# A spectral gate with a token-mixing MLP: two interruptions of the first output pair exchanged

## The chip, the cores and the metric

The kernel runs on one core of one Trainium2 chip. The metric is the device time of one execution in microseconds (us); lower is better. The kernel before has a median of 364.88 us over 3 runs (364.87 to 364.95). The engines are named as the profile names them: PE is TensorE (matmuls; PEld is its weight loads), DVE is VectorE, ACT is ScalarE, POOL is GpSimd, and SP is SyncE, which only issues DMAs.

## The reference

```python
x = A_x                                   # (1, S=2048, D=512)
xn = _layernorm(x, axis=-1)
X = rfft2(xn) * (w_r + 1j * w_i)          # over tokens and channels
s = irfft2(X)                             # (1, 2048, 512)
u = gelu(einsum("bsd,sf->bdf", _layernorm(xn), w1) + b1)    # F = 1792
y = einsum("bdf,fs->bds", u, w2) + b2
g = silu(y.transpose(0, 2, 1))
return x + s * g
```

So there are two branches on the normalised tokens: a two-dimensional Fourier filter `s`, and an MLP across the tokens whose output, through silu, gates it.

## The kernel before, in words

The tokens lie in 16 groups of 128 (`NJ`), each a tile of 128 partitions by 512 channels. The work goes through three stages.

In the first, each group is normalised, the first products of the MLP (`w1` against the tokens, 128x512 matmuls in three passes of high and low parts) run, and between them the transform over the tokens. In the second, the remaining products of `w1` run, and eight steps of the spectral filter (`filter_pair`) are put between them. Its result stays in the tile `ey`, still without the last transform over the channels.

The third stage makes the output, and the change lies there. The 16 output groups are taken as 8 pairs `p`, groups `p` and `p + 8`. Each pair's share of `w2 * u` is a 2x2 block product, and it is made with seven products instead of eight, in the order `ORDER = (1, 2, 5, 6, 3, 7, 4)`. The product `n` (`products`, line 905) is 21 matmuls of 128x128 by 256 columns: three passes (high by high, high by low, low by high) over seven blocks (`FORMS`). The fixed side comes from a weight form `w2f`, of which there are three buffers: ACT copies its high part, DVE makes its low part (`w2_high`, `w2_low`). The moving side is one of the stored forms of `u`, `fa` to `fd`. Products 1, 6, 7 and 4 go to one bank of PSUM (bank 3 for even pairs, bank 2 for odd ones), product 2 to bank 4, products 5 and 3 to bank 5.

Between the products stands the last transform of the spectral branch, in small steps that I call interruptions:

- `gathered` (line 953) copies a pair's columns of `ey` into the tile `yt`, two copies on ACT and two on DVE.
- `even_channels` (line 966) multiplies `yt` with the constants `ci` for the even channels: 16 fp32 matmuls on 64x64 quarters of the array, 32 records in the profile, into the first 256 columns of banks 6 and 7.
- `odd_channels` (line 977) does the same for the odd channels: 4 fp32 matmuls on the full array, 8 records, into the last 256 columns of these banks.
- `unfolded` (line 984) has ACT copy a part of bank 7 and DVE add and subtract the two into `es` and `y`.
- `spectral` (line 1006) is the last step over the tokens: 4 fp32 matmuls on quarters (8 records) from `y` into banks 0 and 1. `finish` multiplies with the gate and adds to the output.

The order of the work is written out by hand: `tc.keep_in_program_order` keeps each engine's instructions as the program issues them. For the loop over `k` (line 1047) `SLOTS` says behind which product a pair's interruption stands (`slot`; 6 for the first pair, which is the seventh product, 5 for most others), and which pieces of `gathered` and `unfolded` follow each product. `PARTS` (line 44) says what the interruption holds and in which order: S is `spectral` of the pair before, E the even channels, O the odd ones. The first pair alone has its transform in two interruptions: line 1074 puts a step behind the sixth product, `k == slot - 1`, and `PARTS[0]` names the one behind the seventh. The second pair and the last have "SEO", the five between them "ESO". `even_channels` and `odd_channels` of a pair write different columns, and `unfolded` comes behind both.

Of the kernel before, what the change touches and what calls it, by code (L numbers as in the profile page):

```python
# [40 lines left out]

PARTS = ("O", "SEO", *["ESO"] * 5, "SEO")

KD = np.concatenate([np.arange(0, 256, 4), np.arange(2, 256, 4), np.arange(1, 256, 2)])

# [94 lines left out]
def spectral_mixer_kernel(tc, x, w1, b1, w2, b2, wk, we, wx, c_f, c_ft, c_d, c_i, c_g, c_h, out):  # L142
# [19 lines left out]
    with tc.tile_pool(name="ps", bufs=1, space=PSUM) as psp, ExitStack() as left, ExitStack() as right:  # L162
# [675 lines left out]
        def sums_of_blocks():  # L838
            added_up("a12", "s1")
            added_up("a11", "a12")  # L840
# [61 lines left out]
        def banks(p):  # L902
            return ps[:, 3 - p % 2, :HD], ps[:, 4, :HD], ps[:, 5, :HD]

        def products(p, n):

            wf = ready.pop(0)
            bx, by, bz = banks(p)
            o = {1: bx, 6: bx, 7: bx, 4: bx, 2: by, 5: bz, 3: bz}[n]

            for a, (wi, ui) in enumerate(((0, 0), (0, 1), (1, 0))):
                for m, i in enumerate(FORMS):
                    T.matmul(o, wf[:, wi, i], form_parts(n, i)[ui], start=m + a == 0 and n in (1, 2, 5),
                             stop=m == NH - 1 and a == 2, skip_group_check=n in (6, 3, 7, 4))

        def copied(name, src, where):
            t = where.tile([P, HD], F32, name=name, tag=name.split("_")[0], bufs=1)
            step(A.activation(t, src, AF.Copy))
            return t
# [25 lines left out]
        def new_gates(p):  # L945
            return [fp.tile([P, D], F32, name=f"g{j}", tag="g", bufs=4) for j in (p, p + NP)]
# [6 lines left out]
        def gathered(p):  # L953


            yt = fp.tile([P, 2, 4, 2, 64], F32, name=f"yt{p}", tag="yt")
            yts[p] = yt
            for i, j in enumerate((p, p + NP)):
                for h in range(2):
                    to = yt[:, i, :, h ^ i].rearrange("p b (s c) -> p b s c", c=2)  # L960
                    yield V.tensor_copy(to, ey[:, :, h::2, j]) if i else A.activation(to, ey[:, :, h::2, j], AF.Copy)

        def tokens_of(yt, i, b):
            return yt[:, i, b].rearrange("p e c -> p (e c)")

        def even_channels(p):


            for i in range(2):
                for s in range(2):  # L970
                    at = slice(128 * i + 64 * s, 128 * i + 64 * s + 64)
                    for e in range(2):
                        for r, rows in enumerate((slice(0, 64), slice(64, P))):
                            T.matmul(ps[64 * e:64 * e + 64, 6 + r, at], yts[p][rows, i, 2 * s, e], ci[rows, 2 * s, :64],
                                     start=True, stop=True)

        def odd_channels(p):

            for i in range(2):
                for s in (1, 0):  # L980
                    at = 256 + 128 * s
                    T.matmul(ps[:, 6 + i, at:at + P], tokens_of(yts[p], i, 2 * s + 1), ci[:, 2 * s + 1], start=True, stop=True)

        def unfolded(p):

            es, y = new_sums(p) if p else first_sums
            e0, e1 = (es[:, :, k].rearrange("p i b c -> p i (b c)") for k in range(2))
            first, odd = ps[:, 6, :256].rearrange("p (i s c) -> p i s c", s=2, c=64), ps[:, 6:8, 256:]
            other = y.rearrange("p i h q c -> p (i h q c)")[:, :257]
            A.activation(other, ps[:, 7, :257], AF.Copy)  # L990
            other = other[:, :256].rearrange("p (i s c) -> p i s c", s=2, c=64)

            V.tensor_add(es[:, :, 1, :, :64], first, other)
            V.tensor_sub(es[:, :, 1, 0, :63:-1], first[:, :, 0], other[:, :, 0])
            V.tensor_sub(es[:, :, 1, 1, :63:-1], other[:, :, 1], first[:, :, 1])
            V.tensor_add(e0, e1, odd)
            V.tensor_sub(e1, e1, odd)
            yield
            u, v = es[:, :, :, 0], es[:, :, :, 1]
            V.tensor_add(y[:, :, :, 0], u, v)  # L1000
            yield
            V.tensor_sub(y[:, :, ::-1, 1], u, v)
            ys[p] = y.rearrange("p i h q c -> p i (h q c)")
            yield

        def spectral(p):

            y = ys.pop(p)
            for e, cols in enumerate((slice(0, 64), slice(64, P))):
                for r, rows in enumerate((slice(0, 64), slice(64, P))):  # L1010
                    i = e ^ r
                    T.matmul(ps[cols, i], cft[rows, cols], y[rows, i], start=True, stop=True)

        def gate(g, j, cols, src, scale):
            A.activation(g[:, cols], src, AF.Silu, bias=b2t[:, j:j + 1], scale=scale)

        def summed(name, a, b):
            t = fp.tile([P, HD], F32, name=name, tag="c", bufs=2)
            V.tensor_add(t, a, b)
            return t  # L1020
# [17 lines left out]
        for p in range(NP):  # L1038
            j0, j1 = p, p + NP
            more = p + 1 < NP  # L1040
            if p:
                gates[p] = new_gates(p)
            g0, g1 = gates[p]
            bx, by, bz = banks(p)
            slot, plan = SLOTS[min(p, 2) + (not more)]
            gathering = gathered(p)
            for k, n in enumerate(ORDER):
                started = not p and k < 2
                if not started:
                    products(p, n)  # L1050
                if n == 1 and p:
                    p1 = copied(f"p1_{p}", bx, w2p)
                elif n == 5:
                    p5 = copied(f"p5_{p}", bz, fp)
                elif n == 6:
                    v2 = copied(f"v2_{p}", bx, fp)
                elif n == 7:
                    c22 = summed(f"c22_{p}", bx, p5)
                if n == 3 and more:
                    c12 = summed(f"c12_{p}", bz, v2)  # L1060
                if not started:
                    ready.extend(w for w in [next(wforms, None)] if w is not None)
                if n == 2:
                    c11 = summed(f"c11_{p}", by, p1)
                elif n == 6:
                    gate(g0, j0, left_, c11, 1.0)
                elif n == 3 and more:
                    gate(g0, j0, right_, c12, 1.0)
                elif n == 7:
                    gate(g1, j1, right_, c22, -1.0)  # L1070
                elif n == 4:
                    for cols in (left_,) if more else quarter_rows:
                        gate(g1, j1, cols, bx[:, cols], -1.0)
                if not p and k == slot - 1:
                    even_channels(p)
                if k == slot:
                    for part in PARTS[p]:
                        {"S": spectral, "E": even_channels, "O": odd_channels}[part](p - (part == "S"))
                    yts.pop(p)
                    pieces = unfolded(p)  # L1080
                    if p:
                        for g, j in zip(gates.pop(p - 1), (j0 - 1, j1 - 1)):
                            finish(g, j, whole)
                for what in plan.get(k, ""):
                    next(gathering if what == "g" else pieces)
                if n == 3 and not more:
                    gate(g0, j0, right_, summed(f"c12_{p}", bz, v2), 1.0)
                if more and n == 7:
                    sums_of_blocks()
                if not more and k == 2:  # L1090
                    xr = [where.tile([P, NH * P], F32, name=f"xr{i}", tag="s1", bufs=1)[:, :D] for i, where in enumerate((w2p, fp))]
                    for to, j in zip(xr, (j0, j1)):
                        for rows, tokens in halved:
                            SY.dma_start(to[rows], x[tokens, j])
                if not more and k == 5:
                    spectral(p)
                    last_rows = fp.tile([P, 2, D], F32, name="rows", tag="yt")
                    finish(g0, j0, whole)
                    finish(g1, j1, right_)
# [38 lines left out]
```

## Time and profile before

| what | value |
|---|---|
| median of 3 runs | 364.88 us (364.87 to 364.95) |
| the profiled execution's own time | 365.01 us |
| its span, first to last instruction | 363.2 us |
| mean granted TensorE clock | 0.996 |
| busy PE, PEld | 357.3 us, 310.4 us |
| busy DVE, ACT, POOL | 307.4 us, 210.8 us, 87.2 us |
| HBM traffic | 59.70 MB read, 8.13 MB written |

A line of the timeline gives the start from the beginning of the span, the length, the engine, the line, the operation with its tiles (output first, then inputs) and how many instructions are merged in it; in brackets stands how long the engine sat idle before it and what ended that. The line is 139 for nearly all, because a helper on that line issues them; so the tiles tell the steps apart. `ps<-fb,w2f` is a product, `ps<-cd,yt 64*64` the even channels, `ps<-cd,yt 128*128` the odd ones, `ps<-y,cft` the step over the tokens. In a merged line the matmuls overlap; the length runs to the end of the last one. Where two kinds of work follow each other with the same tiles, one line holds both ("x40" is 32 records of even and 8 of odd channels).

### The profile page before, as it was taken

To read this page: it belongs to the slowest core of one execution; us is meant where nothing else is said; L and a number is where in the kernel's file an instruction comes from. 1 tells how busy PE (TensorE), PEld (TensorE's weight loads), DVE (VectorE), ACT (ScalarE), POOL (GpSimd) and SP (SyncE) were. 2 spreads that over 40 slices of the span, in tenths; PEclk is the share of its full clock that TensorE was granted. 3 is DMA by queue.
4 is the path that set the end of the run, shared out by engine and by line. 5 is a ranking of instruction groups with operands and counts; after the bars stand their busy time and mean duration, and the time that the engine had idled before them with its cause. 6 is when DMAs were issued, how large, how long until landed. Compare 5 with 4: busy or idle time off the path is not lost.

```text
span 363.2 us, 8851 instructions
## 1 busy us (share of the span) xinstructions
PE 357.3 (98%) x3476; PEld 310.4 (85%) x3476; DVE 307.4 (85%) x590; ACT 210.8 (58%) x385; POOL 87.2 (24%) x134
## 2 busy tenths in 40 slices
PE   8999999999999999999999999999999999999994
PEld 7788888888777788777888999999898989898993
DVE  5899999967799996999995988687887878787974
ACT  4877778867534425756337884646464546565431
POOL 4233333323222022220120001050504132230330
PEclk9999999999999999999999999999999999999998
DMA  7978999306695686996568288698888989898624
GB/s 211 253 181 205 219 289 317 143 0 158 174 264 188 192 249 178 253 239 208 175 213 181 101 227 174 180 188 203 195 192 203 188 216 175 233 151 219 113 27 90
DMA packets 33293, 68.66 MB, mean 189 GB/s; under 512 B 4612, under 2 KB 19380, under 8 KB 33124
## 3 DMA queue, kind: packets, MB, share of 16 engines
q1 hardware_dynamic: 24276, 42.44, 41.2%
q0 software_dynamic: 8496, 25.01, 32.1%
q10 hardware_dynamic: 480, 0.66, 0.6%
q8 instruction: 27, 0.44, 0.5%
q14 instruction: 14, 0.11, 0.1%
HBM read 59.70 MB, written 8.13 MB: 187 GB/s over the span
## 4 chain that ended last, share of the span: by engine, by line
PE 97%; DMA 1%; DVE 1%; ACT 0%; issue 0%; DVEq 0%
PE ps L139 97%; DMA x<-in_x_dram 1%; DVE rows L139 0%; DVE stm L244 0%; DVE h L272 0%; ACT g L139 0%; DVE tm L229 0%; ACT sdm L223 0%; DVEq L1134 0%; DVE mvm L220 0%; DVE rsm L230 0%; DVE r0m L228 0%; DVE v2m L221 0%; DVE v2m L222 0%; DVEq L469 0%
## 5 line engine op out<-in xcount | busy, mean ns | idle before, releaser
L139 PE MATMUL ps<-h,w1h 128*128 128x512 f32 x400 | 116.3, 397 | 0.3 <-DVE h L272 0.3
L139 PEld LDWEIGHTS ps<-h,w1h 128*128 128x128 f32 x400 | 72.9, 188 | 20.1 <-issue 4.9
L139 PE MATMUL ps<-h,w1l 128*128 128x512 f32 x200 | 67.6, 390 | 0.0
L139 DVE TENSOR_TENSOR w2f<-a,w2f 128x896 fp32r<-128x896 f32 x36 | 39.2, 1090 | 16.4 <-ACT w2f L139 16.4
L139 ACT ACTIVATE w2f<-a 128x896 fp32r<-128x896 f32 x36 | 37.1, 1030 | 19.8 <-ACT g L139 8.4
L139 PEld LDWEIGHTS ps<-h,w1l 128*128 128x128 f32 x200 | 37.5, 188 | 8.1
L139 PE MATMUL ps<-fb,w2f 128*128 128x256 f32 x336 | 41.9, 279 | 0.0
L139 POOL DMA_DIRECT2D s<-in_w_dram x14 | 18.3, 1311 | 96.5 <-DVE w2f L139 46.5
L139 PE MATMUL ps<-fa,w2f 128*128 128x256 f32 x336 | 41.2, 277 | 0.0
L139 PEld LDWEIGHTS ps<-fb,w2f 128*128 128x128 f32 x336 | 39.7, 188 | 0.9 <-DVE c L139 0.8
L139 PE MATMUL ps<-fc,w2f 128*128 128x256 f32 x336 | 39.8, 277 | 0.0
L139 PEld LDWEIGHTS ps<-fa,w2f 128*128 128x128 f32 x336 | 39.7, 188 | 0.0
L139 PEld LDWEIGHTS ps<-fc,w2f 128*128 128x128 f32 x336 | 39.0, 188 | 0.0
L155 ACT ACTIVATE w1h<-w1s 128x512 fp32r<-128x512 f32 x26 | 16.2, 631 | 25.1 <-DMA w1s<-in_w_dram 12.0
L139 POOL DMA_DIRECT2D out_dram<-r x28 | 23.6, 1276 | 26.7 <-DVE r L139 26.7
L667 POOL DMA_DIRECT2D xc<-xc x16 | 9.8, 620 | 70.3 <-ACT xc L665 55.1
L308 POOL TENSOR_TENSOR ey<-t 128x256 f32<-128x256 f32 x16 | 15.7, 980 | 44.0 <-DVE t L306 44.0
L139 ACT ACTIVATE w2f<-s 128x896 fp32r<-128x896 f32 x15 | 15.3, 1020 | 14.1 <-PE ps L139 12.3
L139 DVE TENSOR_TENSOR w2f<-s,w2f 128x896 fp32r<-128x896 f32 x15 | 16.3, 1089 | 6.2 <-ACT w2f L139 6.1
L469 DVE TENSOR_TENSOR w1l<-w1r,w1h 128x384 fp32r<-128x384 f32 x32 | 21.3, 670 | 0.0
L268 ACT ACTIVATE h<-x,nbm,rsm 128x256 f32<-128x256 f32 (+1 forms) x34 | 18.4, 591 | 4.2 <-DVE nbm L263 3.2
L139 PE MATMUL ps<-fd,w2f 128*128 128x256 f32 x168 | 20.6, 277 | 0.0
(132 smaller groups left out, 602.1 us busy)
## 6 DMA issues: line engine op xcount, KB each, us to landing
a<-in_w_dram SPq DMA_DIRECT2D x22, 448.0 KB, 4.2
wt<-in_wk_dram POOLq DMA_DIRECT2D x16, 512.0 KB, 6.1
s<-in_w_dram SPq DMA_DIRECT2D x16, 448.0 KB, 4.5
s<-in_w_dram POOLq DMA_DIRECT2D x16, 448.0 KB, 6.7
w1s<-in_w_dram SPq DMA_DIRECT2D x52, 128.0 KB, 5.0
w1r<-in_w_dram SPq DMA_DIRECT2D x28, 192.0 KB, 4.6
xc<-xc POOLq DMA_DIRECT2D x16, 256.0 KB, 3.1
out_dram<-in_x_dram SPq DMA_DIRECT2D x4, 960.0 KB, 6.7
```

The source lines that it names most:

```text
L139: return lambda *args, **kw: self.keep(operation(*args, **kw))
L155: return A.activation(hi, src, AF.Copy), V.tensor_sub(lo, src, hi.bitcast(F32))
L268: keep(A.activation(to, v, AF.Identity, bias=m["nb"][:, i], scale=m["rs"][:, i, 1:2]))
L308: G.tensor_add(ey[:, 0::3, :, j], a, b)
L469: keep(V.tensor_sub(dst, src, hi.bitcast(F32)))
L667: keep(G.dma_start(*(v.rearrange("p s t c -> p s (t c)") for v in (there[c::2], here[1 - c::2, ::-1]))))
```

## The change

The two interruptions of the first pair change places: the odd channels stand behind the sixth product (`n` = 7), the even channels, on the quarters of the array, behind the seventh (`n` = 4). The other pairs, the pieces of `gathered` and `unfolded`, and all other instructions stay as they are.

```diff
-PARTS = ("O", "SEO", *["ESO"] * 5, "SEO")
+PARTS = ("E", "SEO", *["ESO"] * 5, "SEO")
...
                 if not p and k == slot - 1:
-                    even_channels(p)
+                    odd_channels(p)
                 if k == slot:
                     for part in PARTS[p]:
                         {"S": spectral, "E": even_channels, "O": odd_channels}[part](p - (part == "S"))
```

## The prediction

> **What bounds the kernel now.** I read the page of the profile first (busy shares), then the chain that ended last in order of time, then the waits of TensorE (PE in the profile), then PE's timeline through the output stage, and last the other engines around the two places that the change touches.
>
> ```profile
> PE 357.3 (98%) x3476; PEld 310.4 (85%) x3476; DVE 307.4 (85%) x590; ACT 210.8 (58%) x385; POOL 87.2 (24%) x134
> ...
> 199.88 158.78 PE ps L139 x1573
> ...
> PE ps L139 <- POOL wz L443: 1.1, 1, 1.1
> PE ps L139 <- DVE h L272: 0.3, 1, 0.3
> ```
>
> The second line is the chain: from 199.88 us it is PE alone for 158.78 us, through the whole output stage up to 4 us before the end. The last two lines are all that PE waited for by that view, both at the start of the kernel (the zero tile, the first normalised rows). So the time here is the sum of PE's own steps, and a change to the order of two of them counts only if it changes that sum or makes PE wait. PE's timeline around the two interruptions is therefore the place to work from. The columns are start, length, engine, line, operation and count.
>
> ```profile
> 212.56 2.64 PE L139 MATMUL ps<-fa,w2f 128*128 128x256 f32 x21
> 215.03 2.63 PE L139 MATMUL ps<-fb,w2f 128*128 128x256 f32 x21
> 217.59 0.69 PE L139 MATMUL ps<-cd,yt 64*64 64x64 f32 x32
> 218.22 2.74 PE L139 MATMUL ps<-fb,w2f 128*128 128x256 f32 x21
> 220.80 1.05 PE L139 MATMUL ps<-cd,yt 128*128 128x128 f32 x8
> 221.61 2.72 PE L139 MATMUL ps<-fd,w2f 128*128 128x256 f32 x21
> 224.16 2.63 PE L139 MATMUL ps<-fa,w2f 128*128 128x256 f32 x21
> ```
>
> A row of 21 matmuls is one product. Lengths overlap, because matmuls are pipelined, so I take a step's cost from its start to the next step's start. The fifth product (212.56) takes 2.47 us in this way with product on either side: that is a plain product. The sixth takes 2.56, the even channels (32 records on 64x64 quarters) 0.63, the seventh 2.58, the odd channels (8 records on the full array) 0.81, and the first product of the next pair 2.55.
>
> **The change part by part.** The change exchanges the rows at 217.59 and 220.80 and nothing else. No matmul is added or removed, no DMA is issued by either step, and the queues of SP and POOL are not passed: both steps hold matmuls only. VectorE (DVE) and ScalarE (ACT) keep their order.
>
> Step 1, the sum on PE as it is: 2.56 + 0.63 + 2.58 + 0.81 + 2.55 = 9.13 us from 215.03 to 224.16. Three plain products are 3 x 2.47 = 7.41, so the two interruptions cost 1.72. Of that 0.63 + 0.81 = 1.44 is their own; 0.09 lies at the edge into the even channels (2.56 against 2.47), 0.11 in the product between the even and the odd channels (2.58), which I count to the even channels' exit, 0.08 behind the odd channels (2.55).
>
> Step 2, the sum after: each interruption still stands between two products of the same shape, so each keeps its edges: 2.47 + 0.81 + 2.47 + 0.08 + 0.09 + 0.63 + 2.47 + 0.11 = 9.13. The difference is 0.00. The one edge that moves to an unseen neighbour is that behind the even channels, with the first product of the next pair behind it instead of the seventh of this one. Its nearest row is the edge of 0.11 above. Taken from nothing to twice that, the cost is bounded at -0.11 and +0.11; I take 0.00, since the two products have the same shape and count.
>
> Step 3, waits of the moved step. The odd channels now start where the even ones did, 3.21 us earlier (220.80 - 217.59). They read the gathered tile yt, and need both halves of its rows, but so do the even channels.
>
> ```profile
> 214.35 0.78 ACT L139 ACTIVATE yt<-ey 128x256 f32<-128x256 f32 x2
> 215.39 0.54 DVE L139 COPY yt<-ey 128x256 f32<-128x256 f32 x2
> ...
> 221.04 1.05 ACT L139 ACTIVATE w2f<-s 128x896 fp32r<-128x896 f32 x1 [1.86 <-issue]
> ...
> 222.01 0.46 ACT L139 ACTIVATE g<-ps,b2t 128x256 f32<-128x256 f32 x1
> 222.13 1.09 DVE L139 TENSOR_TENSOR w2f<-s,w2f 128x896 fp32r<-128x896 f32 x1
> 222.36 0.37 ACT L139 ACTIVATE y<-ps 128x257 f32<-128x257 f32 x1
> ...
> 229.28 0.68 DVE L139 TENSOR_TENSOR y<-es 128x512 f32<-128x512 f32 x1
> ```
>
> The four copies are over at 215.93 (215.39 + 0.54), 1.66 us ahead of 217.59, so the odd channels find them done. If that cover were gone, each microsecond that the copies are late would be a microsecond of PE.
>
> Step 4, what follows later. The seventh product ended 2.56 + 0.63 + 2.58 = 5.77 us behind 215.03; it will end 2.47 + 0.81 + 2.47 + 0.08 = 5.83 behind it, 0.06 later, or 0.15 if the edge of 0.09 into the even channels is counted in. ACT's copy of a new weight form at 221.04 waits for that product to give back its buffer, since there are three such buffers; behind it on ACT stand the gate at 222.01 and the copy at 222.36 that starts the unfolding. All three slip by at most 0.15. The low half of that form, on DVE, ends at 223.22 (222.13 + 1.09), and by the code's order its product is the third of the next pair. That one and PE's next reader of the unfolded y are in these rows:
>
> ```profile
> 226.64 5.11 PE L139 MATMUL ps<-fc,w2f 128*128 128x256 f32 x42
> ...
> 234.06 2.63 PE L139 MATMUL ps<-fb,w2f 128*128 128x256 f32 x21
> 236.62 1.09 PE L139 MATMUL ps<-y,cft 64*64 64x512 f32 x8
> 237.53 1.73 PE L139 MATMUL ps<-cd,yt 64*64 64x64 f32 x40
> 239.02 2.63 PE L139 MATMUL ps<-fb,w2f 128*128 128x256 f32 x21
> 241.49 2.54 PE L139 MATMUL ps<-fd,w2f 128*128 128x256 f32 x21
> 243.87 2.54 PE L139 MATMUL ps<-fa,w2f 128*128 128x256 f32 x21
> 246.25 4.92 PE L139 MATMUL ps<-fc,w2f 128*128 128x256 f32 x42
> ```
>
> The form has 3.42 us to spare (226.64 - 223.22), the unfolded y 6.66 (236.62 - 229.96). A slip of 0.15 is hidden in both, at no cost. Were those margins gone, PE would wait 0.15.
>
> The sum is 0.00, with -0.11 to +0.11 for the moved edge. Against the profiled execution's own time of 365.01 us (a span of 363.2 and 1.8 around it) it leaves 365.01; that execution stands 0.13 above the median of 364.88, so the forecast in terms of the median is 364.88, given as 364.9.
>
> **The rivals.** The first has to do with a thing in these rows that the sum passes over: the plain product has two prices. Before 236.62 it is 2.47; from 241.49 on it is 2.38 (243.87 - 241.49, and again 246.25 - 243.87). The step between them falls on an interruption, and so does the step back near the end:
>
> ```profile
> 340.07 2.54 PE L139 MATMUL ps<-fa,w2f 128*128 128x256 f32 x21
> 342.45 4.92 PE L139 MATMUL ps<-fc,w2f 128*128 128x256 f32 x42
> 347.30 1.09 PE L139 MATMUL ps<-y,cft 64*64 64x512 f32 x8
> 348.21 1.73 PE L139 MATMUL ps<-cd,yt 64*64 64x64 f32 x40
> 349.70 2.72 PE L139 MATMUL ps<-fa,w2f 128*128 128x256 f32 x21
> 352.26 2.63 PE L139 MATMUL ps<-fb,w2f 128*128 128x256 f32 x21
> 354.89 1.09 PE L139 MATMUL ps<-y,cft 64*64 64x512 f32 x8
> ```
>
> At 340.07 a product is still 2.38 (342.45 - 340.07); at 349.70 it is 2.56, which is 2.47 and the 0.08 behind odd channels. So a product costs about 0.09 us more or less according to how PE came out of the interruption ahead of it, and it stays so until the next one.
>
> The Trainium skill bears on that: its page "TensorE: Matmul & The Clock Gate", section "Back-to-back issue gap", gives one gap for an isolated matmul of 256 columns, N / 2.4 + 2.5 = 109.2 ns, and says that in a real stream weight load and matmul set the spacing together, through a reorder window of 64. The first half by itself would leave no room for two prices and give this rival no chance. This trace disagrees with a single figure (2.47 / 21 = 118 ns and 2.38 / 21 = 113 ns); the second half leaves room for a rhythm that an interruption can set.
>
> Rival 1: the exchanged order sets the quicker rhythm earlier. What speaks for it: at 239.02 the quick rhythm begins with odd channels that are followed directly by a seventh product, and the new order makes just that pairing behind the sixth product of the first pair. Against it: odd channels followed by another product have left it slow (221.61, 349.70), and those at 239.02 come behind other 64x64 work, not behind a product. If it holds from the seventh product of the first pair up to 236.62, 7 products gain 0.09 each: 7 x 0.09 = 0.63, and the time is 364.25. If the even channels, after which it was slow at 218.22, put it back at once, the gain is one product, 0.09, and the time 364.79; I count that under the forecast, in whose range it lies.
>
> Rival 2, slower: the interruption in pair 1 (236.62 to 239.02) turns the rhythm over rather than setting it. The interruption of the same order at 347.30 did turn it from quick to slow. If rival 1's condition holds, so that PE enters 236.62 quick, it would then leave it slow, and the products of the next pairs, whose interruptions have kept the rhythm they found, stay slow until 347.30. That is 1 + 5 x 7 + 4 = 40 products at 0.09, 3.60 lost, less the 0.63 won ahead and 3 x 0.09 = 0.27 if the last interruptions turn it over too: 2.70 slower, 367.58. It decides at the product at 241.49. Against it: the two interruptions of that order stand before different products, so that one setting is as good a reading as one turning over.
>
> Rival 3: the 0.15 of step 4 eats into a margin that I have not seen, and PE waits for a weight form or for y. It would need a margin more than twenty times smaller than the 3.42 above, and would give at most 364.88 + 0.15 = 365.03.
>
> **How the numbers follow.** A measurement of this kernel can tell about 0.2% (0.73 us) from no change. Forecast, no change on PE (364.77 to 364.99): 0.70. Rival 1: 0.19. Rival 2: 0.06. Rival 3: 0.05. The forecast, rival 3 and nearly all of rival 1 lie within 0.73 us. Rival 1 with the edge's best bound comes to 0.63 + 0.11 = 0.74, just beyond, and I give 0.03 to that; slower takes the 0.06 of rival 2 and 0.01 of rival 3 for a price larger than its bound. So faster is 0.03, same 0.90, slower 0.07. The range goes from rival 1's 364.25, rounded down to 364.2, to rival 3's 365.03, rounded up to 365.1, and leaves out rival 2.
>
> **What would show it right or wrong.** Right: in the changed profile the odd channels' row stands near 217.5, the even channels' near 221.0, the first product of the second pair ends as before, so that 224.16 reappears within 0.1, and the plain product is 2.47 up to the second pair's interruption and 2.38 behind it. Rival 1 shows as 2.38 between the two interruptions, or from there up to the second pair's, and a row of 236.62 that comes up to 0.63 earlier. Rival 2 shows as 2.47 at 241.49 and after. Rival 3 shows as a wait of PE for DVE or ACT near 226 or 236. The prediction is wrong if the time differs by more than 0.2%; step 2 is wrong if the five steps from 215.03 no longer sum to 9.13 within 0.11.

## The result and the profile after

The changed kernel is slower: 366.45 us (median of 5 runs, 366.25 to 366.78) against 364.88. The ratio is 1.0041, with a 95% interval of 1.0028 to 1.0053: some 1.5 us, clear of no change. The profiled execution took 366.78 us, with a span of 365.0; that of before 365.01 with 363.2.

The page's busy shares say little: PE is busy 1.4 us longer and its share is 98% as before. The first two lines are from the page, the others from the waits of PE.

```profile
span 365.0 us, 8851 instructions
...
PE 358.7 (98%) x3476; PEld 311.4 (85%) x3476; DVE 307.5 (84%) x590; ACT 211.1 (58%) x385; POOL 87.1 (24%) x134
...
PE ps L139 <- POOL wz L443: 1.1, 1, 1.1
PE ps L139 <- DVE h L272: 0.3, 1, 0.3
PE ps L139 <- DVE c L139: 0.2, 1, 0.2
```

The third wait is new, PE for a sum `c` on DVE. PE's timeline shows where it stands, and the rest of the loss.

```profile
215.07 2.63 PE L139 MATMUL ps<-fb,w2f 128*128 128x256 f32 x21
217.55 1.05 PE L139 MATMUL ps<-cd,yt 128*128 128x128 f32 x8
218.81 2.74 PE L139 MATMUL ps<-fb,w2f 128*128 128x256 f32 x21 [0.22 <-DVE c L139]
221.49 0.69 PE L139 MATMUL ps<-cd,yt 64*64 64x64 f32 x32
222.11 2.74 PE L139 MATMUL ps<-fd,w2f 128*128 128x256 f32 x21
...
234.58 2.63 PE L139 MATMUL ps<-fb,w2f 128*128 128x256 f32 x21
237.15 1.09 PE L139 MATMUL ps<-y,cft 64*64 64x512 f32 x8
238.06 1.73 PE L139 MATMUL ps<-cd,yt 64*64 64x64 f32 x40
239.54 2.72 PE L139 MATMUL ps<-fb,w2f 128*128 128x256 f32 x21
242.10 2.63 PE L139 MATMUL ps<-fd,w2f 128*128 128x256 f32 x21
244.58 2.63 PE L139 MATMUL ps<-fa,w2f 128*128 128x256 f32 x21
...
278.41 1.16 PE L139 MATMUL ps<-cd,yt 128*128 128x128 f32 x8
279.33 2.63 PE L139 MATMUL ps<-fb,w2f 128*128 128x256 f32 x21
281.80 2.54 PE L139 MATMUL ps<-fd,w2f 128*128 128x256 f32 x21
284.18 2.54 PE L139 MATMUL ps<-fa,w2f 128*128 128x256 f32 x21
```

I number the pairs from 0, as the code does. Against before, the start of the step over the tokens in pair 1 is 0.53 late (237.15 against 236.62): 0.05 was there before the interruption (217.55 against 217.50, see e2), and the odd channels with the wait take 1.26 (218.81 - 217.55) where the exchange alone takes 0.81, which is 0.45; the last 0.03 lie in the product behind the wait. Nothing is added up to 239.54 (239.02 before). Then it grows. In before the product is quick, 2.38, from 241.49 on; here it is slow, 2.48 (244.58 - 242.10), and turns quick only behind the interruption of pair 3. These are before's rows there:

```profile
276.59 1.16 PE L139 MATMUL ps<-cd,yt 128*128 128x128 f32 x8
277.50 2.63 PE L139 MATMUL ps<-fb,w2f 128*128 128x256 f32 x21
```

279.33 against 277.50 is 1.83 late, and so it stays: the last product starts 1.81 later (357.72 against 355.91). So 1.83 - 0.52 = 1.31 us went between 239.54 and 279.33, over 14 products: 0.093 each, the difference between the two prices. The granted clock has no part in it: it is 1.00 in that stretch in both kernels (columns: window; its length, PE busy and instructions; granted clock; DMA share; GB/s). First the kernel before, then the changed one.

```profile
241.00:276.00 35.00, 35.00 (x363) 1.00 0.85 194
```

```profile
241.00:276.00 35.00, 35.00 (x325) 1.00 0.82 179
```

In the same 35 us PE is busy throughout, at the same clock. The two counts, 363 and 325, are not the price of a product: most of the 38 more in before are small matmuls of pair 3's interruption, which begins at 275.10 there and at 276.93, outside the window, in the changed kernel. The products alone show it: 279 of their matmuls in 31.84 us of PE's time in before, 277 in 32.67 in the changed kernel, about 114 against 118 ns each.

The wait has its cause in DVE's and ACT's rows.

```profile
216.27 1.03 ACT L139 ACTIVATE w2f<-a 128x896 fp32r<-128x896 f32 x1 [1.09 <-DMA a<-in_w_dram]
217.33 1.09 DVE L139 TENSOR_TENSOR w2f<-a,w2f 128x896 fp32r<-128x896 f32 x1 [1.04 <-ACT w2f L139]
218.34 0.42 DVE L139 TENSOR_TENSOR c<-ps,p 128x256 f32<-128x256 f32 x1
```

The sum `c22` reads bank 3 behind the sixth product, and the seventh goes on accumulating into the same bank, so it has to wait until `c22` has read. `c22` stands on DVE behind the low part of pair 1's first weight form, that behind ACT's copy, and that waited for a weight load until 216.27. In before the load came 0.60 earlier:

```profile
215.67 1.03 ACT L139 ACTIVATE w2f<-a 128x896 fp32r<-128x896 f32 x1 [0.54 <-DMA a<-in_w_dram]
...
217.75 0.42 DVE L139 TENSOR_TENSOR c<-ps,p 128x256 f32<-128x256 f32 x1
```

There `c22` was over at 218.17, 0.05 ahead of the seventh product at 218.22. That 0.05 is no margin: where PE did wait, it started just as far behind the sum's end (here 218.34 + 0.42 = 218.76 and 218.81).

### The profile page after: what moved, and what is told of

Its sections match the earlier page's. It is cut to its first block, busy times and chain, and to the rows that moved or that the text cites. A ratio compares the mean times of both kernels' runs of the same rounds, so it can differ in the third digit from the quotient of the medians.

```text
span 365.0 us, 8851 instructions
## 1 busy us (share of the span) xinstructions
PE 358.7 (98%) x3476; PEld 311.4 (85%) x3476; DVE 307.5 (84%) x590; ACT 211.1 (58%) x385; POOL 87.1 (24%) x134
## 4 chain that ended last, share of the span: by engine, by line
PE 91%; DMA 3%; DVE 2%; ACT 2%; issue 1%; ACTq 1%; DVEq 0%; SPq 0%
PE ps L139 91%; DMA a<-in_w_dram 2%; DMA w1r<-in_w_dram 1%; DVE a L836 1%; ACTq L452 1%; ACT fc L363 0%; ACT h L268 0%; ACT w2f L139 0%; DVE w2f L824 0%; ACT w2f L820 0%; DVE rows L139 0%; DVE h L469 0%; ACT u L355 0%; DVE fc L368 0%; DVE fa L368 0%
```

## The experiments

I call the price that holds from product to product the rhythm: slow at 2.47, quick at 2.38. Three theories stood at the start: the wait for `c22` costs the time and upsets the rhythm too (W+R in the expectations); the order of the two steps sets the rhythm, wait or no wait (O); the wait is chance, a load that lands late, in either kernel (L). The tables come first. The ratio is that to the kernel before, run beside each.

| run | edit | median us | ratio (95%) |
|---|---|---|---|
| e1 | the kernel before | 365.03 | 1.0002 (0.9989 to 1.0016) |
| e2 | the changed kernel | 366.29 | 1.0031 (1.0021 to 1.0042) |
| e3 | changed, `c22` first on DVE | 366.31 | 1.0031 (1.0019 to 1.0043) |
| e4 | odd, even, both behind the sixth product | 366.31 | 1.0030 (1.0019 to 1.0041) |
| n1 | changed, 2 extra matmuls in pair 1 | 368.91 | 1.0104 (1.0089 to 1.0120) |
| n2 | before, 2 extra matmuls in pair 1 | 366.48 | 1.0039 (1.0026 to 1.0051) |
| n3 | changed, 1 extra | 368.73 | 1.0097 (1.0082 to 1.0112) |
| n4 | changed, 3 extra | 365.32 | 1.0005 (0.9996 to 1.0015) |
| v1 | even, odd, both behind the sixth product | 364.94 | 0.9997 (0.9988 to 1.0007) |
| c1 | before, 2 extra at the stage's start | 366.54 | 1.0038 (1.0023 to 1.0053) |
| w1 | pair 0's both behind the sixth product, pairs 1 to 6 even-step-odd, 1 extra | 368.77 | 1.0091 (1.0076 to 1.0107) |
| w2 | the same, 2 extra | 369.01 | 1.0097 (1.0076 to 1.0118) |
| e5 | before, `c22` first on DVE | 364.97 | 0.9991 (0.9979 to 1.0003) |

The second table tests the account. "Shift" is how much later than in before (234.06) pair 1's sixth product starts, with any extra work behind it and any wait at the end; "slow" is how many more slow products than in before follow, up to the end. The very last product counts too: it is slow in before (the row at 355.91 is 2.74 long) and quick in the changed kernel (2.65 at 357.72), so the 14 above are 13 here. The sum is 363.2 + shift + 0.093 x slow.

| run | shift | slow | sum | span |
|---|---|---|---|---|
| after | 0.52 | 13 | 364.9 | 365.0 |
| e1 | 0.46 | 0 | 363.7 | 363.7 |
| e2 | 0.00 | 13 | 364.4 | 364.5 |
| e3 | 0.01 | 14 | 364.5 | 364.5 |
| e4 | 0.11 | 14 | 364.6 | 364.6 |
| v1 | 0.40 | 0 | 363.6 | 363.6 |
| e5 | -0.14 | 0 | 363.1 | 363.1 |
| n1 | 0.04 + 0.18 + 0.17 | 38 | 367.1 | 367.2 |
| n2 | -0.01 + 0.18 | 14 | 364.7 | 364.7 |
| n3 | -0.06 + 0.07 + 0.16 | 38 | 366.9 | 366.9 |
| n4 | 0.07 + 0.29 | -1 | 363.5 | 363.5 |
| c1 | 0.23 | 14 | 364.7 | 364.8 |
| w1 | 0.22 + 0.18 | 37 | 367.0 | 367.1 |
| w2 | 0.23 + 0.17 | 38 | 367.1 | 367.2 |

So the shift and the number of slow products together give every span to 0.1 us, and most of the difference lies in the second. (The fourteenth run, s1, doesn't fit the table; see there.)

**The two kernels again, and the wait taken away.** e1 and e2 are the two kernels unchanged. e3 is the changed kernel with `c22` ahead of that low part on DVE, which takes the wait away by order:

```diff
-                yield w2_form(f"1_{p}", cur["a12"])
+                w = w2_high(f"1_{p}", cur["a12"])
+                if p == 1:
+                    yield
+                yield w2_low(*w)
...
                     c22 = summed(f"c22_{p}", bx, p5)
+                    if not p:
+                        ready.append(next(wforms))
```

> The kernel before once more, for a second profile. Theory W+R (the seventh product waits for DVE's sum c22, and a wait of PE upsets the rhythm of later products): 364.9 us, no wait of PE behind the first matmul stage, the plain product 2.47 us up to pair 1's interruption and 2.38 from there to the last pair. Rival L (the wait only comes from weights that happened to land late, whatever the order): the seventh product waits here as well in some executions, times spread by about 0.5 us.

> The changed kernel once more. W+R: 366.2 to 366.8 us, a wait of the seventh product of pair 0 for DVE of 0.1 to 0.6 us, and the quick rhythm (2.38) beginning in another pair than in its first profile or in the same, since the wait ends at no fixed moment. Rival O (the order of odd and even channels sets the rhythm, wait or no wait): the quick rhythm begins at the same place as in its first profile, pair 3's interruption. Rival L: in an execution with the weights on time 364.9.

> The changed order, but DVE makes the sum c22 ahead of the low part of pair 1's first weight form, so that it no longer stands behind a weight load. W+R: the wait is gone (c22 ends near 218.1, the odd channels at 218.4), 364.9 us with a spread below 0.1, and the rhythm of the kernel before. Rival O: no wait, but the slow rhythm up to pair 2 or 3 stays, 365.6 to 366.3 us. Rival L: 364.9 as well, but so would the changed kernel in e2 with its weights on time.

The timeline of e1, the kernel before:

```profile
216.14 1.03 ACT L139 ACTIVATE w2f<-a 128x896 fp32r<-128x896 f32 x1 [0.93 <-DMA a<-in_w_dram]
...
218.21 0.42 DVE L139 TENSOR_TENSOR c<-ps,p 128x256 f32<-128x256 f32 x1
218.68 2.74 PE L139 MATMUL ps<-fb,w2f 128*128 128x256 f32 x21 [0.31 <-DVE c L139]
```

And PE's timeline of e2, the changed kernel:

```profile
215.03 2.63 PE L139 MATMUL ps<-fb,w2f 128*128 128x256 f32 x21
217.50 1.05 PE L139 MATMUL ps<-cd,yt 128*128 128x128 f32 x8
218.31 2.72 PE L139 MATMUL ps<-fb,w2f 128*128 128x256 f32 x21
220.96 0.69 PE L139 MATMUL ps<-cd,yt 64*64 64x64 f32 x32
221.59 2.74 PE L139 MATMUL ps<-fd,w2f 128*128 128x256 f32 x21
224.17 2.63 PE L139 MATMUL ps<-fa,w2f 128*128 128x256 f32 x21
...
237.53 1.73 PE L139 MATMUL ps<-cd,yt 64*64 64x64 f32 x40
239.02 2.72 PE L139 MATMUL ps<-fb,w2f 128*128 128x256 f32 x21
241.58 2.63 PE L139 MATMUL ps<-fd,w2f 128*128 128x256 f32 x21
244.06 2.63 PE L139 MATMUL ps<-fa,w2f 128*128 128x256 f32 x21
```

The wait changes sides: the kernel before has it here, the changed kernel hasn't. With it e1 is as quick behind pair 1 as before; without it e2 and e3 (whose waits name no `c`) are as slow as the changed kernel was. So the wait comes and goes with the landing of a load, as L has it, costs its own 0.4 us or so, and isn't what made the difference: W+R, and L too, gave 364.9 for a changed kernel free of the wait, and it took 366.3. e2 shows that difference bare: 224.17, 237.53 and 239.02 stand where before has 224.16, 237.53 and 239.02, and then one product takes 2.56 where it took 2.47. From pair 1 on both programs give PE the same instructions with the same operands.

**Order or place.** Is it the order, odd before even? e4 puts both steps behind the sixth product in that order, v1 in the other one, with nothing behind the seventh:

```diff
-PARTS = ("E", "SEO", *["ESO"] * 5, "SEO")
+PARTS = ("", "SEO", *["ESO"] * 5, "SEO")
...
                 if not p and k == slot - 1:
                     odd_channels(p)
+                    even_channels(p)
```

(v1 has `even_channels(p)` ahead of `odd_channels(p)`.)

> Odd and then even channels both behind the sixth product, none behind the seventh. The cover of the sum c22 is then 0.81 + 0.6 us. W+R: no wait, or one below 0.1, 364.8 to 364.9 us (one edge of 0.1 fewer), small spread. Rival O: no wait, slow rhythm up to pair 2 or 3, 365.5 to 366.2. Rival L: 364.8.

> No extra matmul: even and then odd channels of pair 0, both behind the sixth product. The sum c22 has 1.5 us of cover. Theory G: no forecast of the pair of turning from the order alone; the time is 364.8 + 0.093 for each slow product more, or less, than in the kernel before (364.3 if the quick rhythm begins behind this interruption, 364.9 in pair 1, 366.2 in pair 3, 368.7 never). Rival O (odd ahead of even is what costs): even ahead of odd, so as the kernel before, 364.8 to 364.9.

e4 has no wait for `c` either and turns quick at pair 3 like the changed kernel, v1 at pair 1 like the one before. Had these been the last runs, "the odd channels must come last" would have looked shown. It was not, as the next runs tell.

**A few matmuls more.** If the order as such sets the rhythm, a little extra work on PE ahead of pair 1's interruption leaves it alone. The extra matmuls are 128x128 by 128 columns, with forms at hand; their result is read by nothing:

```diff
+        def nudge(n, m, wf):
+            for _ in range(m):
+                T.matmul(ps[:, 4, HD:HD + P], wf[:, 0, FORMS[0]],
+                         form_parts(n, FORMS[0])[0][:, :P], start=True, stop=True, ...)
...
                 if k == slot:
+                    nudge(n, NUDGE.get((p, "x"), 0), last[0])
                     for part in PARTS[p]:
```

Theory G in the expectations is a guess of mine from the starts in the traces: the moment at which PE enters an interruption, taken on a grid of a few nanoseconds, decides how it leaves. `NUDGE` gives the number of extra matmuls for pair 1 (n1 and n2: 2, n3: 1, n4: 3); c1 has 2 ahead of pair 0's first product instead. n2 and c1 are the kernel before otherwise, n1, n3 and n4 the changed one.

> The changed order, with two extra 128-column matmuls on the full array (their result is used by nobody) behind the sixth product of pair 1, ahead of that pair's interruption. Theory G (the rhythm after an interruption depends on the moment at which PE enters it, on a fine grid of some 6.7 ns; in e1 to e4 that moment followed from the order alone, wait or no wait): two matmuls at a start distance of about 111.7 ns shift the moment by 3.3 ns on that grid, which is what separates the quick from the slow case of pair 1, so the quick rhythm begins in pair 1, about 14 products gain 0.093 each, 1.3 less 0.22 for the two: 365.1 to 365.3 us. Rival O (the order of odd and even channels in pair 0 keeps it slow up to pair 3 by itself): 366.2 + 0.2 = 366.4 to 366.5 us.

> The order of before, with the same two extra matmuls at the same place. Theory G: pair 1 now comes out of its interruption slow, as in the changed kernel, and the quick rhythm begins some pairs later: 364.9 + 0.2 + up to 1.3, so 365.7 to 366.4 us. Rival O: quick from pair 1 as before, 364.9 + 0.2 = 365.1 us.

> The changed order with one extra matmul of 128 columns (result unused) ahead of pair 1's interruption, where n1 had two and stayed slow from pair 1 to pair 6. Theory G (the moment of entry on a fine grid sets the rhythm): another moment, so another pair in which the quick rhythm begins, or none; the time is 364.9 + 0.15 for the extra matmul + 0.093 for each slow product more than the kernel before has, between 365.0 and 368.9 us, and differs from the 366.4 that the extra matmul alone would make of the changed kernel, unless the moment happens to lead to pair 3 again. Rival O (the order by itself keeps it slow up to pair 3): 366.4 us.

> The same with three extra matmuls. Theory G: again its own pair of turning, 365.3 to 369.1 us, by 364.9 + 0.38 + 0.093 for each further slow product. Rival O: 366.65 us.

> The order of before with two extra matmuls ahead of the very first product of the output stage. Theory G: the moment of the whole stage is shifted, so the pair of turning may be another one, and the first products may be quick from the start: 365.1 if nothing turns, 363.9 if the 13 products ahead of pair 1's interruption become quick and the rest stays, 366.4 to 367.5 if they do but pair 1 leaves slow. Rival O: 365.1.

PE's timeline behind pair 1's interruption in n2, the kernel before with two matmuls more:

```profile
239.18 2.72 PE L140 MATMUL ps<-fb,w2f 128*128 128x256 f32 x21
241.74 2.63 PE L140 MATMUL ps<-fd,w2f 128*128 128x256 f32 x21
244.22 2.63 PE L140 MATMUL ps<-fa,w2f 128*128 128x256 f32 x21
...
278.96 2.63 PE L140 MATMUL ps<-fb,w2f 128*128 128x256 f32 x21
281.43 2.54 PE L140 MATMUL ps<-fd,w2f 128*128 128x256 f32 x21
```

And in n4, the changed kernel with three:

```profile
241.84 2.54 PE L140 MATMUL ps<-fd,w2f 128*128 128x256 f32 x21
244.22 2.54 PE L140 MATMUL ps<-fa,w2f 128*128 128x256 f32 x21
```

The old order with two extra matmuls has the changed kernel's rhythm, 2.48 up to pair 3; the new order with three has the old kernel's, 2.38 (244.22 - 241.84), and is 1 us faster than the changed kernel although it does 0.3 us more (its shift). One or two in the new order leave the rhythm slow through pair 6, 38 products more than before: 368.7 and 368.9. The order as such doesn't set the rhythm; a small alteration ahead of an interruption can set it or upset it. O misses all five, by 1.3 us or more. G names no number for n3 and n4, and both lie in its wide ranges; of its definite statements n2's came true (366.48, a little above its range), n1's failed (365.1 to 365.3, quick from pair 1; it took 368.91), and c1 fits none of its three cases: its time, 366.54, lies in the range of the third, but its first products stayed slow, and pair 1 left its interruption slow all the same.

**A scan.** s1 puts one to three such matmuls ahead of every product of the kernel before, by pair, to see which shifts lead where.

> The order of before, with one to three extra 128-column matmuls ahead of every product (1 in pairs 0, 3, 4 and 7, 2 in pairs 1 and 5, 3 in pairs 2 and 6; their result is used by nobody). One look, for the rhythm of each of the 56 products. Theory G: the rhythm now changes at product boundaries with no interruption there, in both directions, by the moment at which a product starts; the time has no meaning, about 364.9 + 103 x 0.11 = 376 us. Rival O: the rhythm changes at interruptions only.

It took 416.61 us: the bank that the extra matmuls write to is also read by DVE's sums, and PE waited 24.4 us for them, about half of what the run is longer by; the time means nothing and no table of shifts came out of it. One thing can be read from PE's timeline:

```profile
230.38 2.94 PE L140 MATMUL ps<-fd,w2f 128*128 128x128 f32 x23
233.17 2.86 PE L140 MATMUL ps<-fa,w2f 128*128 128x128 f32 x23
...
245.65 2.77 PE L140 MATMUL ps<-fa,w2f 128*128 128x128 f32 x23
248.26 2.77 PE L140 MATMUL ps<-fb,w2f 128*128 128x128 f32 x23
```

The second group takes 2.61 (248.26 - 245.65), the first 2.79 (233.17 - 230.38): 2.71 without the 0.08 behind odd channels, 0.10 more for as many instructions, at a granted clock of 1.00 in both places. No interruption lies between them, only products with their extra matmuls and a wait of 2.70 us for a sum. So an interruption isn't the only thing that can change the rhythm.

**A forecast that failed.** With the starts of all runs so far theory G gives sharper forecasts for kernels not yet run. w1 and w2 join pair 0's two steps behind the sixth product, give pairs 1 to 6 the order even, step over the tokens, odd, and put one or two extra matmuls ahead of pair 0's interruption.

```diff
-PARTS = ("E", "SEO", *["ESO"] * 5, "SEO")
+PARTS = ("", *["ESO"] * 6, "SEO")
...
                 if not p and k == slot - 1:
+                    nudge(n, NUDGE.get((p, "y"), 0), last[0])
+                    even_channels(p)
                     odd_channels(p)
```

> A version built on theory G: pair 0's even and odd channels both behind the sixth product, one extra 128-column matmul (result unused) ahead of them, and pair 1's interruption in the order ESO like pairs 2 to 6. By the starts in the traces, on a grid of 6.67 ns measured from the quick stretch, a product behind odd channels ran quick when its first matmul stood near 6.0, and the one extra matmul moves it by about -1 from the 0.3 that v1 showed, so to 6.0; ESO entered quick came out quick in every pair seen, SEO entered quick came out slow in the last pair each time. G with that step: quick from pair 1's first product, 7 products more, 364.9 + 0.15 - 0.65 = 364.4 us. G with the step missed: turning in some other pair, 365.0 to 369 us. Rival O: 365.0.

> The same with two extra matmuls, for the size of the step: by the step of about -1 the first matmul stands near 5 on the grid, where products have run slow; slow into pair 1, 365.2 us or more (up to 369), 364.5 if the quick place is wider than the traces show.

Both stayed slow through pair 6, at 368.77 and 369.01, with n1 and n3 the slowest but for s1. w1's sharp forecast, quick from pair 1 and 364.4, is 4.4 us off; the range beside it, 365.0 to 369, takes in nearly everything. w2 was to be slow into pair 1, 365.2 up to 369, and was, at the very end of that range. Twice, in n1 and in w1, G said that the quick rhythm begins in pair 1, and both times it was wrong; so I drop it, though these runs don't exclude every form of it. PE's timeline of w1, behind pair 1's interruption and at the end:

```profile
239.25 2.72 PE L140 MATMUL ps<-fb,w2f 128*128 128x256 f32 x21
241.80 2.64 PE L140 MATMUL ps<-fd,w2f 128*128 128x256 f32 x21
...
353.62 2.63 PE L140 MATMUL ps<-fa,w2f 128*128 128x256 f32 x21
356.08 2.54 PE L140 MATMUL ps<-fb,w2f 128*128 128x256 f32 x21
```

Pair 7's interruption, behind which before turns slow, turned this one quick: 356.08 - 353.62 = 2.46 is 2.38 and the 0.08 behind odd channels. In all profiles but s1's pair 7's interruption turned the rhythm over, from quick to slow or from slow to quick.

**The wait taken from the kernel before.** e5 is e3's edit in the kernel before, to see whether the wait that e1 showed is worth anything.

> The order of before, with the sum c22 made ahead of the low part of pair 1's first weight form, as in e3. W (the wait of the seventh product for c22, seen in one of two profiles of before): no wait in the profile and a narrower spread than the 0.5 us of before, median 364.9 or a little under. If the wait costs nothing: the same spread and median as before.

364.97 against 365.17 beside it, 0.9991 with an interval that holds 1: not to be told from nothing; nor is the spread narrower (364.82 to 366.40, beside it 364.89 to 366.76). Its profile lists no wait for `c`, though the sum still ends only 0.06 ahead of the seventh product (217.69 + 0.42 = 218.11 and 218.17), and its product behind the even channels is quick for once, 2.49 (220.66 - 218.17), which is 2.38 and the edge of 0.11:

```profile
218.17 2.65 PE L139 MATMUL ps<-fb,w2f 128*128 128x256 f32 x21
220.66 1.05 PE L139 MATMUL ps<-cd,yt 128*128 128x128 f32 x8
```

No version beats the kernel before by more than can be measured; v1 and e5 are level with it.

## Why the prediction was wrong, point by point

It said 364.9, with 364.2 to 365.1, and 0.90 for no change; it came to 366.45. What failed is not the sum but what I took to lie outside it. (One reading was a little off too: the chain of PE ends 4.6 us before the end of the span, not 4.)

- **Step 1 and step 2, the sum of 9.13 and no change in it:** right. In e2, free of the wait, the five steps from 215.03 come to 224.17 - 215.03 = 9.14, and the edges moved as written: 2.47, 0.81, 2.65, 0.63, 2.58. The edge behind the even channels, bounded at 0.11 either way, cost the same 0.11 in its new place: 2.58 is 2.47 and 0.11. The profiled changed kernel gives 224.69 - 215.07 = 9.62, for the wait.
- **Step 3, waits of the moved step:** the odd channels found `yt` ready, as written. But I followed only what the moved step reads, not what the product behind it has to wait for. That `c22` reads the seventh product's bank and ends 0.05 ahead of it, no margin at all, was in the trace of before. It cost 0.45 in one profile of the changed kernel and 0.37 in one of the kernel before (e1: 218.68 - 217.68 = 1.00 for even channels that take 0.63), so it belongs to neither order.
- **Step 4, the slip:** right and small; 237.53 and 239.02 didn't move in e2, and its waits of PE name neither `y` nor `w2f`.
- **The step that failed** is the one from those five steps to the whole: from "The difference is 0.00" to "it leaves 365.01". It takes every product behind pair 1's interruption at its price of before, since nothing there is changed. The price of a product isn't a property of the product or its place. It was 2.38 there in one program and 2.47 in the other, for the same instructions. I had seen the two prices and made rivals of them, but priced the forecast's own products as if their rhythm were theirs, and gave 0.70 to that.
- **Rival 1**, the quick rhythm earlier, did not happen: 218.31 to 220.96 is 2.65, slow.
- **Rival 2** (0.06) had the right place and sign: it decided at pair 1's interruption, behind which the product is 2.48 instead of 2.38. Its condition was wrong, that PE enters quick: it entered slow (237.15 - 234.58 = 2.57, a slow product with its edge) and left slow. Its size was wrong too. It took the interruptions even-step-odd to keep the rhythm they find; they keep a quick one in every profile but s1's (where pair 5 goes in quick and comes out slow), but a slow one turned quick at pair 3 in six of ten. So 14 products lost 0.093, 1.30, rather than 40 losing 3.60. That larger loss exists: n1, n3, w1 and w2 have 37 or 38 more slow products.
- **Rival 3** happened in kind, a wait of PE behind a thin margin, but at another place (218, not 226 or 236) and not through the slip.

The Trainium skill's section "Back-to-back issue gap" (page "TensorE: Matmul & The Clock Gate") gives one gap for 256 columns, 109.2 ns for a matmul by itself. The rows of the same 21 instructions give 2.38 / 21 = 113 and 2.47 / 21 = 118 ns, both above it. That in a real stream weight load and matmul set the spacing together, as it also says, agrees with that; no run here shows the reorder window through which, by the page, they do so.

**What stays open:** what sets the rhythm where PE leaves an interruption. Shown is that it is set there (in s1 at another break), that in all profiles but s1's it then holds to the next interruption, and that one to three small matmuls, or the order of two steps 20 us earlier, can tip it. From 224.16 to 239.02 the starts of e2 and before agree to 0.01 us, so the deciding thing is finer than these views; my one reading of it failed. An extra matmul changes two things at once, the moment and the number of instructions behind which PE enters, and no run separates them. What speaks against the moment on a coarse scale: before and e1, one program, enter pair 1's interruption 0.47 us apart (236.62 and 237.09) and both leave quick; the changed kernel and e2 enter 0.53 apart and both leave slow. Open too is how often the kernel before takes the slower path by itself: of its 82 runs on record 7 took 366.3 to 366.8 (366.71 and 366.82 in e1, the others among the runs beside the experiments), about what a turn at pair 3 would give, and none of these was profiled. The 13 of the changed kernel took 366.19 to 366.78, none of them the quicker path.

## What to carry to other kernels

Where one engine is busy throughout, look whether like groups of its instructions have more than one price, and put the whole stretch at the second price, as far as the next place where it changed, into the range: here 14 products at 0.093 outweighed every edge that I had costed. A gain or loss of this kind followed no reason that these runs could find in the edit, so before an order of steps is kept or dropped for it, run the same order with a matmul or two more ahead of it. And follow each product into its accumulating bank: a sum that reads it on another engine is a wait, and its margin is to be read like any other.

## What the runs showed of the hardware that was not expected

- The same stream of weight loads and matmuls (128x128 by 256 columns, no waits, granted clock 1.00) runs at 113 or 118 ns a matmul and stays there for up to 53 products (n1 and n3: all from the stage's start to pair 7's interruption).
- Extra work can make the kernel faster: 3 extra matmuls took the changed kernel from 366.29 to 365.32, while 1 or 2 took it to 368.73 and 368.91.
- The copy that waits for a weight load started at 215.67 and 216.14 in two profiles of the kernel before, and at 216.27 in the changed kernel; the later ones are enough to make PE wait 0.37 and 0.45.
